# Sixteen neighbouring rows per partition: longer runs in HBM for a two-stage attention and highway kernel

## The chip, the cores and the metric

The kernel runs on one core of a Trainium2 chip. The metric is the device time of one execution in microseconds, the median of three runs. The core's engines are TensorE (PE, with its weight loads shown as PEld), VectorE (DVE), ScalarE (ACT), GpSimd (POOL) and SyncE (SP). Sixteen DMA engines move data between HBM and the on-chip memory; POOL and SP each issue transfers on a queue of their own.

## The reference

There are four batches of N = 6336 rows with C = 256 channels. Attention runs over channels, not over rows, so the score matrix of a batch is 256 x 256:

```python
qn = q / (norm(q, axis=1) + 1e-06)          # over the 6336 rows
kn = k / (norm(k, axis=1) + 1e-06)
s = kn.transpose(0, 2, 1) @ qn / tau        # 256 x 256 for each batch
a = softmax(s, axis=-1)
x = (v @ a).reshape(4 * 6336, 256)
H = maximum(x @ w_h, 0)
T = 1 / (1 + exp(-(x @ w_t + b_t)))
out = T * H + (1 - T) * x
```

The scores and the norms are sums over all rows of a batch. In the second half every row of v gives one row of the output, and no row depends on another.

## The kernel before

The rows of a batch are cut into 50 tiles of up to 128 rows, one row to a partition; the last tile has 64. Tiles are gathered into groups of `GS` = 16, so a batch has groups of 16, 16, 16 and 2 tiles. `_load_group` loads a group into an on-chip tile of 128 partitions x 16 x 256. The inputs are float32 and the on-chip tiles float16, and the transfer converts. For a full group it is one transfer of 2 MB read and 1 MB written. For the group of two tiles, one of which is not full, there is one transfer for each tile. All loads are issued on POOL's queue. The tiles of q and k have four buffers each, and those of v three.

A batch has three stages. Stage one (L120 to L149) runs over all tiles and adds up k'q, and the 128 x 128 diagonal blocks of k'k and q'q, in two PSUM banks: six matmuls for each tile. Stage two (L151 to L248) turns this into the normalized scores, their softmax and its product with the two weight matrices: short instructions that hand over between DVE, ACT and TensorE. Then the loads of q and k of the next batch and of its first v group are written (L250 to L252). Stage three (L254 to L395) takes the tiles in pairs. It transposes v on TensorE (L284), copies the transposed pair out of PSUM on DVE or ACT in turn (L296, L301), multiplies it with the prepared matrices (L329, L336, L343), and combines the results: a sigmoid and two rectifications on ACT (L354, L366), two subtractions on DVE (L370), a multiplication on POOL (L378) and a last subtraction on DVE (L382) into the output tile `ostg`, of which there are two buffers. The v load of a group is written one group ahead. A group's output goes out in two halves of `OGS` = 8 tiles: `_store_group` issues each as one transfer on SP's queue, and the last group's as one for each tile.

The order in which an engine runs its instructions is not that of the text alone: the framework (`TileContext`) orders each engine's instructions when the kernel is built, by its own estimate and by the order of the text, and puts in the semaphores. Each engine then runs its list in that order. POOL's list holds all load issues and the multiplications of stage three.

Of the kernel before, what the change touches and what calls it, by code (L numbers as in the profile page):

```python
# [15 lines left out]
P = 128  # L16
# [3 lines left out]
def kernel(  # L20
# [11 lines left out]
    nc = tc.nc  # L32
# [9 lines left out]
    def rows_of(s):  # L42
        return last_rows if s == nsub - 1 else P
# [4 lines left out]
    s = 0  # L48
    while s < nsub:
        ns = min(GS, nsub - s)  # L50
# [21 lines left out]
        out=wht[:, :, 0:C], in_=moe_w_h.rearrange("(kt jl) m -> jl kt m", kt=2)  # L72
    )
    nc.gpsimd.dma_start(
        out=wht[:, :, C : 2 * C], in_=moe_w_t.rearrange("(kt jl) m -> jl kt m", kt=2)
# [13 lines left out]
    def load_qk(bb):  # L89
        for gi, (s0, ns) in enumerate(groups):  # L90
            qt = stream_pool.tile(
                [P, ns, C], f16, tag="q_in", bufs=4, name=f"q{bb}_{gi}"
            )
            kt_ = stream_pool.tile(
                [P, ns, C], f16, tag="k_in", bufs=4, name=f"k{bb}_{gi}"
            )
            _load_group(nc, qt, q[bb], s0, ns, rows_of)
            _load_group(nc, kt_, k[bb], s0, ns, rows_of)
            q_tiles[(bb, gi)] = qt
            k_tiles[(bb, gi)] = kt_  # L100

    def load_v(bb, gi):
        s0, ns = groups[gi]
        vt = stream_pool.tile([P, ns, C], f16, tag="v_in", bufs=3,
                              name=f"v{bb}_{gi}")
        _load_group(nc, vt, v[bb], s0, ns, rows_of)
        v_tiles[(bb, gi)] = vt
# [4 lines left out]
    for b in range(B):  # L112
        ob = out[b * N : (b + 1) * N]
# [6 lines left out]
        for gi, (s0, ns) in enumerate(groups):  # L120
            qt = q_tiles.pop((b, gi))
            kt_ = k_tiles.pop((b, gi))
            for si in range(ns):
                s_idx = s0 + si
                nr = rows_of(s_idx)
# [33 lines left out]
        for idx, (c, off) in enumerate(  # L159
# [3 lines left out]
                out=junk[:, idx, :],  # L163
# [13 lines left out]
        for c in range(2):  # L177
            nc.vector.tensor_scalar(
                out=dcat[:, c, :],
# [12 lines left out]
        for c in range(2):  # L192
            nc.vector.scalar_tensor_tensor(
                out=t1[:, c, :],
# [10 lines left out]
            out=rs, in_=araw, axis=mybir.AxisListType.X, op=AluOp.add  # L205
# [3 lines left out]
        for c in range(2):  # L209
            nc.vector.tensor_scalar(  # L210
                out=mr[:, c, 0:C],
# [20 lines left out]
        for jk in range(2):  # L232
            nc.scalar.copy(
                out=at_sb[:, jk, :].rearrange("p (ic i) -> p ic i", ic=2),
                in_=atps[:, :, jk, :],
# [74 lines left out]
        for pi in range(len(pairs)):  # L310
            if pi + LOOKAHEAD < len(pairs):
                emit_transpose(pi + LOOKAHEAD)
            gi, s0, si, pn, nrows = pairs[pi]
            vt_sb = vtsb_tiles.pop(pi)
            ostg = ostg_tiles[gi]
            ns = groups[gi][1]
# [4 lines left out]
            for u in range(pn):  # L321
                nr = nrows[u]
# [32 lines left out]
                out=uu[0:nr0, 0:pn, :],  # L355
                in_=p3b[0:nr0, 0:pn, :],
# [7 lines left out]
            for u in range(pn):  # L364
                nr = nrows[u]
                nc.scalar.activation(  # L366
                    out=hh[0:nr, u, :], in_=p3a[u][0:nr, C : 2 * C],
# [3 lines left out]
                    out=dd[0:nr, u, :],  # L371
# [7 lines left out]
                out=pp[0:nr0, 0:pn, :], in0=uu[0:nr0, 0:pn, :],  # L379
# [3 lines left out]
                out=ostg[0:nr0, si : si + pn, :], in0=hh[0:nr0, 0:pn, :],  # L383
# [4 lines left out]
            if si + pn >= ns:  # L388
                o0 = 0
                while o0 < ns:  # L390
                    on = min(OGS, ns - o0)
                    _store_group(nc, ob, ostg, s0, o0, on, rows_of)
                    o0 += on
                del ostg_tiles[gi]
                v_tiles.pop((b, gi))  # L395


def _load_group(nc, tile_ap, src2d, s0, ns, rows_of):
    full = all(rows_of(s0 + i) == P for i in range(ns))
    if full:  # L400
        nc.gpsimd.dma_start(  # L401
            out=tile_ap[:, 0:ns, :],
            in_=src2d[s0 * P : (s0 + ns) * P, :].rearrange("(s p) c -> p s c", p=P),
        )
    else:
        for i in range(ns):
            nr = rows_of(s0 + i)
            nc.gpsimd.dma_start(
                out=tile_ap[0:nr, i, :],
                in_=src2d[(s0 + i) * P : (s0 + i) * P + nr, :],  # L410
            )


def _store_group(nc, dst2d, tile_ap, s0, o0, on, rows_of):
    full = all(rows_of(s0 + o0 + i) == P for i in range(on))
    base = (s0 + o0) * P
    if full:
        nc.sync.dma_start(
            out=dst2d[base : base + on * P, :].rearrange("(s p) c -> p s c", p=P),
            in_=tile_ap[:, o0 : o0 + on, :],  # L420
        )
    else:
        for i in range(on):
            nr = rows_of(s0 + o0 + i)
            nc.sync.dma_start(
                out=dst2d[base + i * P : base + i * P + nr, :],
                in_=tile_ap[0:nr, o0 + i, :],
            )

# [2 lines left out]
_INS = ['q', 'k', 'v', 'tau', 'moe_w_h', 'moe_w_t', 'moe_b_t']  # L432
_OUTS = [((25344, 256), 'float32')]
#: Inputs that are plain numbers.
_NUMBERS = {'tau': 1.0}


# [26 lines left out]
```

## Time and profile before

| | before |
|---|---|
| time, median of 3 runs | 414.38 us (414.25 to 415.24) |
| span of the profiled execution | 412.4 us, 6770 instructions |
| PE / PEld busy | 297.5 us (72%) / 212.1 us (51%) |
| DVE busy | 208.9 us (51%) |
| ACT busy | 183.3 us (44%) |
| POOL busy | 189.2 us (46%) |
| load queue (q0) | 77568 packets, 39.20 MB written |
| store queue (q1) | 25856 packets, 25.95 MB |

The profile is of one execution. For this execution it gives the span from the first to the last instruction, 412.4 us; its whole time is not recorded apart from the runs' median, which is 2.0 us longer than the span. Busy shares are means over stages that have different limits, so they don't say by themselves what sets the time. In the rows below, a line such as `93.17 0.61 PE L284 MATMUL vtps<-ident,v ... [10.51 <-DMA v<-in_v_dram]` says that at 93.17 us TensorE began matmuls of line 284, which read the tile `v`, after it had stood idle for 10.51 us, and that a transfer into `v` ended the wait.

### The profile page before, as it was taken

To read this page: it belongs to the slowest core of one execution; us is meant where nothing else is said; L and a number is where in the kernel's file an instruction comes from. 1 tells how busy PE (TensorE), PEld (TensorE's weight loads), DVE (VectorE), ACT (ScalarE), POOL (GpSimd) and SP (SyncE) were. 2 spreads that over 40 slices of the span, in tenths; PEclk is the share of its full clock that TensorE was granted. 3 is DMA by queue.
4 is the path that set the end of the run, shared out by engine and by line. 5 is a ranking of instruction groups with operands and counts; after the bars stand their busy time and mean duration, and the time that the engine had idled before them with its cause. 6 is when DMAs were issued, how large, how long until landed. Compare 5 with 4: busy or idle time off the path is not lost.

```text
span 412.4 us, 6770 instructions
## 1 busy us (share of the span) xinstructions
PE 297.5 (72%) x2637; PEld 212.1 (51%) x2637; DVE 208.9 (51%) x426; ACT 183.3 (44%) x407; POOL 189.2 (46%) x173
## 2 busy tenths in 40 slices
PE   0186839809877899968777999777778938776770
PEld 0176737506544698544445986444447815444440
DVE  0000103707876704497767232887766144786663
ACT  1000126605655306756555055566552166655561
POOL 9212322634646634555548441557366002754453
PEclk9999969957999999999999999999999968999996
DMA  7999999999962999999439999494329700433333
GB/s 95 198 199 197 198 198 199 197 233 188 195 193 70 217 245 198 197 222 241 124 103 173 238 205 198 94 209 138 109 67 215 163 0 0 113 102 103 103 102 121
DMA packets 103456, 65.57 MB, mean 159 GB/s; under 512 B 1537, under 2 KB 103425, under 8 KB 103425
## 3 DMA queue, kind: packets, MB, share of 16 engines
q0 software_dynamic: 77568, 39.20, 70.3%
q1 hardware_dynamic: 25856, 25.95, 20.6%
q8 instruction: 20, 0.33, 0.3%
q14 instruction: 12, 0.09, 0.1%
HBM read 78.38 MB, written 25.95 MB: 253 GB/s over the span
## 4 chain that ended last, share of the span: by engine, by line
PE 24%; DMA 24%; DVE 23%; POOL 17%; issue 7%; ACT 4%; POOLq 0%; DVEq 0%; ACTq 0%
POOL pp L378 15%; DVE o L382 14%; DMA k<-in_k_dram 14%; DVE dd L370 7%; PE p3a L336 7%; DMA v<-in_v_dram 6%; PE sg L129 5%; DMA q<-in_q_dram 4%; PE p3b L329 3%; PE sg L136 2%; PE sg L143 2%; PE vtps L284 2%; ACT hh L366 2%; PE p3b L343 1%; DVE vtsb L296 1%
## 5 line engine op out<-in xcount | busy, mean ns | idle before, releaser
L378 POOL TENSOR_TENSOR pp<-uu,dd 128x512 f32<-128x512 f32 (+1 forms) x104 | 131.4, 1273 | 144.0 <-DVE dd L370 64.8
L336 PE MATMUL p3a<-mr,vtsb 128*128 128x512 f16 (+1 forms) x400 | 134.7, 385 | 33.6 <-DVE dd L370 33.5
L382 DVE TENSOR_TENSOR o<-hh,pp 128x512 f32<-128x512 f32 (+1 forms) x104 | 94.4, 923 | 52.3 <-POOL pp L378 52.3
L366 ACT ACTIVATE hh<-p3a 128x256 f32<-128x256 f32 x200 | 76.1, 386 | 87.1 <-PE p3a L336 57.5
L129 PE MATMUL sg<-q,k 128*128 128x256 f16 (+1 forms) x400 | 94.7, 281 | 25.0 <-DMA k<-in_k_dram 24.1
L329 PE MATMUL p3b<-mr,vtsb 128*128 128x256 f16 (+1 forms) x400 | 100.3, 276 | 0.6 <-ACT uu L354 0.5
L370 DVE TENSOR_TENSOR dd<-hh,p3a 128x256 f32<-128x256 f32 x200 | 75.4, 413 | 29.2 <-ACT hh L366 29.0
L136 PE MATMUL sg<-k 128*128 128x128 f16 (+1 forms) x400 | 89.8, 225 | 0.0
L143 PE MATMUL sg<-q 128*128 128x128 f16 (+1 forms) x400 | 89.7, 224 | 0.0
L296 DVE CAST vtsb<-vtps 128x512 f16<-128x512 f32 (+1 forms) x52 | 34.5, 664 | 98.4 <-PE vtps L284 98.1
L284 PE MATMUL vtps<-ident,v 128*128 128x128 f16 (+1 forms) x400 | 41.1, 222 | 34.9 <-DVE vtsb L296 22.7
L336 PEld LDWEIGHTS <-vtsb 128*128 128x128 f16 (+1 forms) x400 | 39.3, 99 | 42.4 <-issue 18.9
L329 PEld LDWEIGHTS <-vtsb 128*128 128x128 f16 (+1 forms) x400 | 39.3, 99 | 42.2 <-issue 26.7
L354 ACT ACTIVATE uu<-p3b 128x512 f32<-128x512 f32 (+1 forms) x104 | 59.8, 579 | 0.1
L284 PEld LDWEIGHTS <-v 128*128 128x128 f16 (+1 forms) x400 | 30.8, 99 | 54.2 <-issue 32.6
L129 PEld LDWEIGHTS <-k 128*128 128x128 f16 (+1 forms) x400 | 40.2, 100 | 30.5 <-DMA k<-in_k_dram 29.9
L343 PE MATMUL p3b<-btb,ident 128*128 128x256 f16 x200 | 55.2, 276 | 0.0
L143 PEld LDWEIGHTS <-q 128*128 128x128 f16 (+1 forms) x400 | 40.2, 101 | 6.9 <-issue 1.1
L301 ACT CAST vtsb<-vtps 128x512 f16<-128x512 f32 (+1 forms) x52 | 29.3, 563 | 29.2 <-PE vtps L284 29.2
L153 ACT COPY ssb<-sg 128x512 f32<-128x512 f32 x8 | 4.3, 589 | 84.7 <-PE sg L143 84.7
L136 PEld LDWEIGHTS <-k 128*128 128x128 f16 (+1 forms) x400 | 40.2, 101 | 1.7 <-issue 1.4
L401 POOL DMA_DIRECT2D k<-in_k_dram x12 | 14.1, 1176 | 27.9 <-PE sg L143 23.5
(44 smaller groups left out, 123.2 us busy)
## 6 DMA issues: line engine op xcount, KB each, us to landing
out_dram<-o SPq DMA_DIRECT2D x24, 1024.0 KB, 5.4
q<-in_q_dram POOLq DMA_DIRECT2D x12, 1024.0 KB, 19.6
k<-in_k_dram POOLq DMA_DIRECT2D x12, 1024.0 KB, 17.4
v<-in_v_dram POOLq DMA_DIRECT2D x12, 1024.0 KB, 18.0
out_dram<-o SPq DMA_DIRECT2D x4, 128.0 KB, 9.6
q<-in_q_dram POOLq DMA_DIRECT2D x4, 64.0 KB, 23.1
k<-in_k_dram POOLq DMA_DIRECT2D x4, 64.0 KB, 22.6
v<-in_v_dram POOLq DMA_DIRECT2D x4, 64.0 KB, 4.5
```

The costliest lines, as they stand in the source:

```text
L129: nc.tensor.matmul(sg[c][:, 0:C], kt_[0:nr, si, bass.ts(c, P)], qt[0:nr, si, :], start=first, stop=False,)
L136: nc.tensor.matmul(sg[c][:, C : C + P], kt_[0:nr, si, bass.ts(c, P)], kt_[0:nr, si, bass.ts(c, P)], start=False, stop=False,)
L143: nc.tensor.matmul(sg[c][:, C + P : C + 2 * P], qt[0:nr, si, bass.ts(c, P)], qt[0:nr, si, bass.ts(c, P)], start=False, stop=last,)
L284: nc.tensor.matmul(vtps[:, u, c, 0:nr], vt_in[0:nr, si + u, bass.ts(c, P)], ident[0:nr, 0:nr], start=(pcnt == 0), stop=(pcnt == 2 * pn - 1),)
L329: nc.tensor.matmul(p3b[0:nr, u, :], vt_sb[:, u, kt, 0:nr], mr[:, kt, 2 * C : 3 * C], start=(kt == 0 and u == 0), stop=False,)
L336: nc.tensor.matmul(pa[0:nr, :], vt_sb[:, u, kt, 0:nr], mr[:, kt, 0 : 2 * C], start=(kt == 0), stop=(kt == 1),)
L343: nc.tensor.matmul(p3b[0:nr, u, :], ident[:, 0:nr], btb, start=False, stop=(u == pn - 1),)
L354: nc.scalar.activation(out=uu[0:nr0, 0:pn, :], in_=p3b[0:nr0, 0:pn, :], func=Act.Sigmoid, scale=-1.0,)
L366: nc.scalar.activation(out=hh[0:nr, u, :], in_=p3a[u][0:nr, C : 2 * C], func=Act.Relu,)
L370: nc.vector.tensor_tensor(out=dd[0:nr, u, :], in0=hh[0:nr, u, :], in1=p3a[u][0:nr, 0:C], op=AluOp.subtract,)
L378: nc.gpsimd.tensor_tensor(out=pp[0:nr0, 0:pn, :], in0=uu[0:nr0, 0:pn, :], in1=dd[0:nr0, 0:pn, :], op=AluOp.mult,)
L382: nc.vector.tensor_tensor(out=ostg[0:nr0, si : si + pn, :], in0=hh[0:nr0, 0:pn, :], in1=pp[0:nr0, 0:pn, :], op=AluOp.subtract,)
```

## The change

For a full group, partition p now holds the 16 neighbouring rows 16p to 16p + 15 of the group, where it held the rows p, 128 + p, 256 + p and so on. In HBM a partition's share of a load is then one run of 16 KB instead of 16 runs of 1 KB. A store still takes half of the tile, eight of the 16 slots, so each partition writes one run of 8 KB instead of eight of 1 KB. For that `_store_group` is given the group's size `ns`, and a store is contiguous only when the whole group is full. The group of two tiles keeps its transfers of one row to a partition. Tiles on the chip keep their shape and their names, and no instruction of TensorE, DVE or ACT is changed.

```diff
@@ -389,7 +389,7 @@
-                    _store_group(nc, ob, ostg, s0, o0, on, rows_of)
+                    _store_group(nc, ob, ostg, s0, ns, o0, on, rows_of)
@@ -400,7 +400,7 @@
         nc.gpsimd.dma_start(
             out=tile_ap[:, 0:ns, :],
-            in_=src2d[s0 * P : (s0 + ns) * P, :].rearrange("(s p) c -> p s c", p=P),
+            in_=src2d[s0 * P : (s0 + ns) * P, :].rearrange("(p s) c -> p s c", p=P),
         )
@@ -411,19 +411,20 @@
-def _store_group(nc, dst2d, tile_ap, s0, o0, on, rows_of):
-    full = all(rows_of(s0 + o0 + i) == P for i in range(on))
-    base = (s0 + o0) * P
+def _store_group(nc, dst2d, tile_ap, s0, ns, o0, on, rows_of):
+    full = all(rows_of(s0 + i) == P for i in range(ns))
     if full:
+        grp = dst2d[s0 * P : (s0 + ns) * P, :].rearrange("(p s) c -> p s c", p=P)
         nc.sync.dma_start(
-            out=dst2d[base : base + on * P, :].rearrange("(s p) c -> p s c", p=P),
+            out=grp[:, o0 : o0 + on, :],
             in_=tile_ap[:, o0 : o0 + on, :],
         )
     else:
         for i in range(on):
             nr = rows_of(s0 + o0 + i)
+            r0 = (s0 + o0 + i) * P
             nc.sync.dma_start(
-                out=dst2d[base + i * P : base + i * P + nr, :],
+                out=dst2d[r0 : r0 + nr, :],
                 in_=tile_ap[0:nr, o0 + i, :],
             )
```

## Rows read from the trace of the kernel before

**Rows 1.** The page, 40 slices: DMA share in tenths, GB/s moved

```profile
DMA  7999999999962999999439999494329700433333
GB/s 95 198 199 197 198 198 199 197 233 188 195 193 70 217 245 198 197 222 241 124 103 173 238 205 198 94 209 138 109 67 215 163 0 0 113 102 103 103 102 121
```

**Rows 2.** Chain that ended last, 0 to 140 us: start, us, what

```profile
9.44 30.47 DMA k<-in_k_dram
...
41.57 25.91 DMA k<-in_k_dram
...
67.78 25.34 DMA v<-in_v_dram
```

**Rows 3.** Stretches: length, busy us of each engine, PEclk, DMA share, GB/s

```profile
10.00:20.00 10.00, 1.22 (x9) 1.03 (x10) 0.00 (x0) 0.00 (x0) 2.82 (x5) 1.00 1.45 197
...
60.00:70.00 10.00, 8.69 (x95) 6.69 (x94) 3.61 (x10) 5.53 (x10) 2.33 (x2) 0.99 1.46 198
...
84.00:92.00 8.00, 0.00 (x0) 0.00 (x0) 0.00 (x0) 0.00 (x0) 1.92 (x2) 0.50 1.29 244
...
122.00:124.00 2.00, 1.73 (x13) 1.02 (x11) 1.21 (x3) 1.51 (x5) 0.80 (x2) 1.00 1.04 348
```

**Rows 4.** The page, DMA queues and HBM

```profile
q0 software_dynamic: 77568, 39.20, 70.3%
q1 hardware_dynamic: 25856, 25.95, 20.6%
q8 instruction: 20, 0.33, 0.3%
...
HBM read 78.38 MB, written 25.95 MB: 253 GB/s over the span
```

**Rows 5.** Waits from 0 to 100 us: total, times, longest

```profile
PE sg L129 <- DMA k<-in_k_dram: 24.1, 4, 12.3
...
PE vtps L284 <- DMA v<-in_v_dram: 10.5, 1, 10.5
```

**Rows 6.** TensorE's timeline: group 1, first and last of 96 matmuls; first behind v

```profile
29.37 0.28 PE L129 MATMUL sg<-q,k 128*128 128x256 f16 x1 [1.51 <-DMA k<-in_k_dram]
...
36.39 0.22 PE L143 MATMUL sg<-q 128*128 128x128 f16 x1
...
93.17 0.61 PE L284 MATMUL vtps<-ident,v 128*128 128x128 f16 x4 [10.51 <-DMA v<-in_v_dram]
```

**Rows 7.** POOL's timeline: start, us, instruction, count, [idle before <- releaser]

```profile
3.74 1.21 POOL L401 DMA_DIRECT2D q<-in_q_dram  x1
...
67.78 1.15 POOL L401 DMA_DIRECT2D v<-in_v_dram  x1 [3.93 <-DMA k<-in_k_dram]
...
79.86 1.21 POOL L401 DMA_DIRECT2D k<-in_k_dram  x1 [0.75 <-PE sg L136]
...
134.67 1.21 POOL L401 DMA_DIRECT2D v<-in_v_dram  x1
135.90 1.28 POOL L378 TENSOR_TENSOR pp<-uu,dd 128x512 f32<-128x512 f32 x1
...
345.41 1.26 POOL L378 TENSOR_TENSOR pp<-uu,dd 128x512 f32<-128x512 f32 x1 [28.35 <-ACT uu L354]
...
407.18 0.72 POOL L378 TENSOR_TENSOR pp<-uu,dd 64x256 f32<-64x256 f32 x1 [1.35 <-DVE dd L370]
```

**Rows 8.** Waits from 100 us to the end: total, times, longest

```profile
PE sg L129 <- DMA q<-in_q_dram: 0.7, 1, 0.7
...
PEld L284 <- DMA v<-in_v_dram: 0.2, 1, 0.2
```

**Rows 9.** Groups by line, POOL's issues: busy us, mean ns

```profile
L401 POOL DMA_DIRECT2D v<-in_v_dram x12 | 14.5, 1207 | 17.7 <-DMA q<-in_q_dram 9.8 <-PE p3b L343 4.0 <-DMA k<-in_k_dram 3.9
...
L408 POOL DMA_DIRECT2D v<-in_v_dram x8 | 4.6, 576 | 1.9 <-PE p3b L343 1.9
```

**Rows 10.** The page, DMA issues: count, KB each, us to landing

```profile
out_dram<-o SPq DMA_DIRECT2D x24, 1024.0 KB, 5.4
```

## The prediction

> **What bounds the kernel now.** I read the 40 slices of the page first. From the second to the eighth, some 10 to 82 us, the rate stands at 197 to 199 GB/s; after that it moves up and down [rows 1]. So the run has two parts. The chain that ended last says the same: from 9 to 93 us it consists of three long pieces that are waits for loads (30.5, 25.9 and 25.3 us), and the last of them is a v load [rows 2].
>
> The stretches give the rate. With loads alone it is 197 to 198 GB/s, and the DMA share doesn't move [rows 3]. These are bytes written as f16; HBM reads are 78.4 MB where the load queue moves 39.2 MB [rows 4], so the loads read about 396 GB/s. One load of a full group writes 1.049 MB and thus takes 1.049 / 0.198 = 5.30 us.
>
> Which load sets the end of this part? The waits of TensorE: until 100 us it waits 24.1 us for k in four waits (the longest, 12.3, ahead of the first matmul) and 10.5 us for v [rows 5]. That v wait ends at 93.17 us [rows 6], and in the 8 us before it no engine but POOL does anything [rows 3]. It is the v of group 1 of batch 0, issued at 67.78 us, the 15th full-group load in POOL's queue [rows 7], behind all of q and k of batch 1. Check: 15 loads of 5.30 are 79.5 us; the eight single-tile loads of the two last groups (0.39 MB) 2.0 us; one store that passes between them 3.4 us (84 to 92 us moved 244 GB/s, 1.95 MB; less a store of 1.05 that leaves 0.90 of loads where 1.58 would have passed alone, and the missing 0.68 MB are 3.4 us [rows 3]). That is 84.9 us; with the first issue at 3.74, 4.5 us remain for the weights, the first descriptors and the last landing. So the time of this landing is 15 times the time of one load plus about 13.6 us.
>
> After 100 us TensorE waits 0.7 us for q and its weight loads 0.2 us for v, in all [rows 8]. The other 320 us are matmuls and the chain of ACT, DVE and POOL, with loads far ahead. What the change gains or loses is therefore read between 4 and 93 us; later, loads and stores are covered by arithmetic.
>
> **The change part by part.** Bytes, instruction counts of the engines, tile shapes and waits stay: sums over rows don't care which partition holds which row, and v's rows go out in the order in which they came in. Only the runs in HBM change.
>
> *Loads.* A full group was 2048 runs of 1 KB and is 128 of 16 KB. The trace has no load of such runs, so I bound it by the nearest rows. The only packets of about that size are those of the instruction queue q8: 20 packets, 0.33 MB, 0.3% of 16 engines' span [rows 4]. Before rounding 0.25 to 0.35% of 16 x 412.4 us are 16.5 to 23.1 us, or 0.82 to 1.15 us a packet, 0.99 in the middle. The load queue had 77568 packets in 70.3%, 59.8 ns each, 0.957 us for sixteen. So by this row a load takes between 0.82 / 0.957 = 0.86 and 1.21 times its present time, 4.57 to 6.40 us. Parity is in the middle of that, but q8's few packets fell between those of the busy load queue and carry waits for it, while whatever a packet costs by itself is paid by the loads 2048 times and would be paid 128 times. I take the middle between parity and the favourable end, 0.93: 4.92 us. For 15 loads that is 15 x 0.38 = 5.7 us (bounds: 11.0 gained, 16.5 lost).
>
> [...]
>
> *Issues on POOL.* A full-group issue holds POOL 1.21 us, one of 128 or 64 runs 0.58 [rows 9]. If runs set this, each of 36 issues gets about 0.6 us shorter. Before the first load of the chain that is worth 0.6 us (bound: nothing, if descriptors are used while they are still written). Later it matters only where a multiplication of the third stage starts right behind an issue, as at 134.67 and 135.90 us [rows 7]; there are five such places, up to 3.0 us, but the multiplications behind them soon wait for DVE again. I take 0.5.
>
> *Stores.* Runs of 8 KB for 1 KB. A store is 5.4 us from issue to landing [rows 10], and where one passed alone the queues moved 348 GB/s [rows 3]. The buffer it empties is wanted two groups later; the 25 pairs of the last batch take from 345 to 408 us [rows 7], so a group of eight pairs is some 20 us. Nothing waits for them but the one that crosses the loads at 84 us (3.4 us, which could halve or vanish if the v load lands first; I take nothing). The last stores belong to the group of two tiles, which keeps its 1 KB rows. Cost and gain nothing; without the cover of the arithmetic one store would be worth its 3 us.
>
> *Queues.* POOL is the queue of all loads and of the multiplications; an issue there that blocks holds both. No wait is added. Behind the v load, the next late thing would be the v of group 2, wanted some 20 us later and issued at once behind it, with one k load between: 10 us, so it is not late.
>
> Sum: 5.7 + 0.6 + 0.5 = 6.8 us. The profiled span is 412.4 us, and the median of the runs 414.4: 2.0 us lie around the span and stay. 412.4 - 6.8 = 405.6, and 407.6 as a run.
>
> **Rivals.**
>
> *The runs stay short, or their length doesn't matter.* If the transfer is still cut at each row of 256 elements, nothing changes: 414.4. If runs are long but the read rate was at its limit, only POOL's 1.1 us remain: 413.3. For it: the load rate is so flat that it looks like a ceiling [rows 1, 3], and no row shows a higher one for reads. Against: a fixed cost of each packet gives a rate that is as flat. [...]
>
> *Long packets are slower* (the other side). If the middle of q8's row is right, a load takes 0.99 / 0.957 of 5.30 = 5.48 us, and 15 x 0.18 - 1.1 = 1.6 us are lost: 416.0; at its far end 6.40 us, 16.5 - 1.1 lost: 429.8. Place: the same v landing. It decides slower from 5.46 us a load (1.24 + 1.1 = 2.34 us over 15). For it: the row itself; against: its waits among the loads.
>
> *The order of instructions changes.* The framework orders each engine's work ahead of time: a k load of batch 2 stands at 79.86 us among the multiplications of batch 0 [rows 7], though the text has it a batch later. If its estimate of a load depends on runs, the order moves. TensorE stands idle for over 10 us before the v landing, and the 16 tiles of a group in stage one take 7.0 us (29.37 to 36.39) [rows 6]: one group of batch 1 moved into that gap would give 7 more, 400.6. The other way, work that now fills a wait moves out of it and the saving is eaten: 412 to 418.
>
> **How the numbers follow.** The trace speaks for the first part's bound and for little else, so most of the chance lies there; the row of q8, read at its middle, keeps the slow case alive, and for a change of the order no row gives a sign, only a place where it would pay more than it could cost. A load between 4.57 and 5.22 us in the present order: 0.62, about 402.3 to 412.1, likeliest 407.6 and mostly 404.5 to 410. No effect: 0.15. Slower packets: 0.08. A better order: 0.10. A worse one: 0.05. A measurement of this kernel tells 0.3%, 1.24 us, from no change. Faster: 0.62 + 0.10 = 0.72. Same: 0.15 + 0.02 of the worse order = 0.17. Slower: 0.11. The range of 402 to 414.4 us holds the first case, the second and little else, about 0.78.
>
> **What would show it.** The load rate between 10 and 80 us: right if near 213 GB/s, wrong if still 198 or below. Packets of the load queue: some 8,400 in place of 77,568 (36 x 128, the single-tile loads' rows, the weights and completions), and of the store queue some 4,400 in place of 25,856; if they stay, the runs were cut. POOL's issues near 0.6 us. The v wait of TensorE should end near 87 us, and everything behind it should stand about 6 us earlier in the same order; if the distance from that landing to the end is not some 319 us, the order or the third stage moved, and the sum is wrong there. TensorE's waits for loads after 100 us should stay below 1 us; if they grow, transfers I counted as covered aren't.

## The result, and the profile after

The changed kernel takes 402.94 us (median, 402.27 to 404.79) beside 414.31 us for the kernel before (414.04 to 415.24), measured together: a ratio of 0.973, 95% interval 0.970 to 0.976. That is 11.4 us faster, inside the range that was forecast, 4.7 us below the forecast time of 407.6 and below the stretch of 404.5 to 410 in which it was mostly expected. The profiled execution took 402.83 us; its span is 401.1 us, 11.3 less than before.

The page of the kernel after: the DMA share and rate in 40 slices, the load and store queues, HBM's bytes, and the stores' time from issue to landing.

```profile
DMA  7999999997726999993229996553259100322223
GB/s 117 215 217 212 213 217 215 214 263 149 251 105 138 302 212 212 220 276 118 109 57 255 264 217 130 141 176 115 106 108 287 47 0 0 116 105 108 105 105 124
...
q0 software_dynamic: 8448, 39.20, 49.5%
q1 hardware_dynamic: 4352, 25.95, 16.2%
...
HBM read 78.38 MB, written 25.95 MB: 260 GB/s over the span
...
out_dram<-o SPq DMA_DIRECT2D x24, 1024.0 KB, 4.7
```

The bytes are those of [rows 4], and the packets of the load queue fell from 77568 to 8448: the runs really are long. The flat part of the rate is there as in [rows 1], but at 212 to 217 GB/s.

Stretches of the kernel after (length, busy us of PE, PEld, DVE, ACT and POOL, granted clock, DMA share, GB/s):

```profile
10.00:20.00 10.00, 3.39 (x25) 2.89 (x26) 0.00 (x0) 0.00 (x0) 1.09 (x2) 1.00 1.02 214
...
60.00:70.00 10.00, 9.53 (x85) 6.63 (x83) 3.39 (x9) 6.59 (x14) 1.80 (x2) 1.00 1.05 219
...
84.00:92.00 8.00, 7.62 (x40) 4.68 (x41) 5.36 (x9) 3.38 (x8) 2.24 (x2) 0.63 1.03 237
```

Beside [rows 3] the loads' rate is 214 to 219 where it was 197 and 198, 215 in the mean from 10 to 80 us. A load of 1.049 MB so takes 4.88 us where it took 5.30. The third line shows what that did: from 84 to 92 us TensorE now works 7.62 us, where it stood still before.

The chain that ended last (start, us, what) and TensorE's waits up to 100 us (total, times, longest), after:

```profile
6.39 29.95 DMA k<-in_k_dram
...
37.39 24.80 DMA k<-in_k_dram
...
62.47 21.86 DMA v<-in_v_dram
```

```profile
PE sg L129 <- DMA k<-in_k_dram: 20.4, 3, 10.1
...
PE vtps L284 <- DMA v<-in_v_dram: 6.1, 1, 6.1
```

The same three loads hold the first part as in [rows 2]. The waits have shrunk from 24.1 to 20.4 us and from 10.5 to 6.1 us [rows 5]: the loads still set the end of this part, by less.

TensorE's timeline after, at its first matmul of stage one and at the end of the v wait:

```profile
16.61 0.39 PE L129 MATMUL sg<-q,k 128*128 128x256 f16 x1 [10.08 <-DMA k<-in_k_dram]
...
84.38 0.61 PE L284 MATMUL vtps<-ident,v 128*128 128x128 f16 x4 [6.14 <-DMA v<-in_v_dram]
```

The first matmul stood at 18.79 us before, the end of the v wait at 93.17 [rows 6]. So 2.18 us come before any matmul, 8.79 us are there by the v landing, and the last 2.5 of the 11.3 us arise behind it. To place those I use the matmul of L187, which runs once in stage two of every batch. It stood at 61.73, 158.63, 244.97 and 333.01 us before, and stands at 57.31, 149.74, 235.02 and 321.19 now. From the v landing to the second of them is 65.46 us before and 65.36 after; to the third 86.34 and 85.28; to the fourth 88.04 and 86.17; to the end 79.39 and 79.91. TensorE's timeline at the two ends of the middle stages, before and then after:

```profile
158.63 0.27 PE L187 MATMUL cqb<-dcat,ones2d 128*128 128x256 f16 x1
...
333.01 0.27 PE L187 MATMUL cqb<-dcat,ones2d 128*128 128x256 f16 x1
```

```profile
149.74 0.27 PE L187 MATMUL cqb<-dcat,ones2d 128*128 128x256 f16 x1
...
321.19 0.27 PE L187 MATMUL cqb<-dcat,ones2d 128*128 128x256 f16 x1
```

The two middle stages got 2.93 us shorter. TensorE waits for one load there, the q of [rows 8], before and not after:

```profile
250.65 0.27 PE L129 MATMUL sg<-q,k 128*128 128x256 f16 x1 [0.65 <-DMA q<-in_q_dram]
```

From one instruction to the same one in the kernel after, 0.62 of the 2.93 us are gained at this wait; where the rest is gained is seen under e4_long_early.

The last stage hides gains and a loss. The last store is issued 75.37 us behind L187 before and 74.33 after; it lands 3.10 us after its issue before and 2.52 after, behind the last store of 8 KB runs; and from there to the end of the span it is 0.92 us before and 3.02 after. What is waited for there is a DRAIN that GpSimd's queue runs at the end of the program. The last lines of the two kernels, L459 before and L460 after (count, ns min/median/max, first and last start):

```profile
L459 POOLq DRAIN  x3: 51/102/1972, 407.2 to 412.1; - x3
```

```profile
L460 POOLq DRAIN  x3: 51/102/5975, 394.3 to 400.8; - x3
```

The long one is the first of the three. Before, it ends at 409.13 us, 2.3 ahead of the last store's landing; after, it ends at 400.27, 2.2 behind that landing, and the closing instructions of all engines follow only then, from 400.32 us on. The change thus loses 2.1 us at the end of the run.

What is gained up to the v landing divides by the completions of the loads in the trace. From the first k load to the v of batch 1 (twelve full-group loads and the eight small ones) it is 65.62 us before and 61.30 after: 4.32. From there to the v load that ends the wait, with one store crossing, it is 8.76 us and 6.47: 2.29, of which 0.42 is one load's rate. The store's crossing itself thus costs 3.46 us before and 1.59 after.

The trace also has the completion of each of the 16 DMA engines, and what waits for a load starts with the last of them: the first matmul 0.05 us behind it before and 0.04 after (18.74 and 16.57 us at the first k load), the matmul behind the v wait 0.05 and 0.04 (93.12 and 84.34 us). By the mean of the 16, the first load completes at 12.36 us before and 11.33 after, the first k load at 17.64 and 16.19, and the v of batch 1 at 83.53 and 77.01. So from the k to that v 5.07 us are gained, 12 x 0.42, and 6.52 in all. The last engine trails the mean by 1.10 us before and 0.38 after at the first k load, and by 0.83 and 0.86 at that v: of the 2.18 us at the first matmul 0.7 are the last engine's and are lost again on the way, which is why the completions of the last engine give 4.32 and not 5.07.

### The profile page after: what moved, and what is told of

It is laid out like the page before. It is cut to its first block, busy times and chain, and to the rows that moved or that the text cites. A ratio compares the mean times of both kernels' runs of the same rounds, so it can differ in the third digit from the quotient of the medians.

```text
span 401.1 us, 6770 instructions
## 1 busy us (share of the span) xinstructions
PE 295.7 (74%) x2637; PEld 211.2 (53%) x2637; DVE 206.1 (51%) x426; ACT 183.6 (46%) x407; POOL 167.8 (42%) x173
## 3 DMA queue, kind: packets, MB, share of 16 engines
q0 software_dynamic: 8448, 39.20, 49.5%
## 4 chain that ended last, share of the span: by engine, by line
PE 30%; DVE 23%; DMA 19%; POOL 16%; issue 5%; ACT 5%; POOLq 0%; DVEq 0%; ACTq 0%
POOL pp L378 15%; DVE o L382 14%; DMA k<-in_k_dram 14%; PE sg L129 7%; DVE dd L370 7%; PE p3a L336 7%; DMA v<-in_v_dram 5%; PE sg L136 4%; PE sg L143 4%; PE p3b L329 3%; PE vtps L284 2%; ACT hh L366 2%; DVE vtsb L296 1%; PE p3b L343 1%; PE ahat L241 1%
## 5 line engine op out<-in xcount | busy, mean ns | idle before, releaser
L378 POOL TENSOR_TENSOR pp<-uu,dd 128x512 f32<-128x512 f32 (+1 forms) x104 | 132.5, 1283 | 146.2 <-DVE dd L370 68.3
L382 DVE TENSOR_TENSOR o<-hh,pp 128x512 f32<-128x512 f32 (+1 forms) x104 | 91.4, 895 | 52.2 <-POOL pp L378 52.2
L129 PE MATMUL sg<-q,k 128*128 128x256 f16 (+1 forms) x400 | 93.7, 279 | 20.8 <-DMA k<-in_k_dram 20.4
L370 DVE TENSOR_TENSOR dd<-hh,p3a 128x256 f32<-128x256 f32 x200 | 75.6, 414 | 28.3 <-ACT hh L366 28.3
L343 PEld LDWEIGHTS <-ident 128*128 128x128 f16 x200 | 19.7, 99 | 3.9
```

The source lines that it names most:

```text
L129: nc.tensor.matmul(sg[c][:, 0:C], kt_[0:nr, si, bass.ts(c, P)], qt[0:nr, si, :], start=first, stop=False,)
L343: nc.tensor.matmul(p3b[0:nr, u, :], ident[:, 0:nr], btb, start=False, stop=(u == pn - 1),)
L370: nc.vector.tensor_tensor(out=dd[0:nr, u, :], in0=hh[0:nr, u, :], in1=p3a[u][0:nr, 0:C], op=AluOp.subtract,)
L378: nc.gpsimd.tensor_tensor(out=pp[0:nr0, 0:pn, :], in0=uu[0:nr0, 0:pn, :], in1=dd[0:nr0, 0:pn, :], op=AluOp.mult,)
L382: nc.vector.tensor_tensor(out=ostg[0:nr0, si : si + pn, :], in0=hh[0:nr0, 0:pn, :], in1=pp[0:nr0, 0:pn, :], op=AluOp.subtract,)
```

## The experiments

Theory A is that the load rate sets the time to the v landing, that the stores are covered, and that whatever is gained later comes from POOL's shorter issues. The expectations name the rivals. Every kernel was timed beside the kernel before on the same chip; "before" is 414.0 to 414.4 us in each case.

### Loads alone, stores alone

Kernel before with long loads only, and kernel after with its loads put back. In these two, in e3_long_late, e4_long_early and e13_first_two_short loads and stores place some rows differently, so rows of the output stand at other places; bytes and instruction counts are the same.

```diff
# e1_long_loads: before, in _load_group
-            in_=src2d[s0 * P : (s0 + ns) * P, :].rearrange("(s p) c -> p s c", p=P),
+            in_=src2d[s0 * P : (s0 + ns) * P, :].rearrange("(p s) c -> p s c", p=P),
# e2_long_stores: after, in _load_group
-            in_=src2d[s0 * P : (s0 + ns) * P, :].rearrange("(p s) c -> p s c", p=P),
+            in_=src2d[s0 * P : (s0 + ns) * P, :].rearrange("(s p) c -> p s c", p=P),
```

> All full-group loads in 16 KB runs, stores as before in 1 KB rows, so rows of v leave at other places than they should. Theory A (the saving is made by the loads: 6.3 us of load rate and 1.3 us of the start before the v landing, 2.5 us of shorter issues on POOL after it, and 1.2 us where the one store crosses the loads): 403 to 404.5 us, the v wait ends at 84.5 to 86 us, and 316.7 us follow it. Theory B (the 2.5 us after the landing come from the stores' longer runs): 405.5 us or more, and 319 us follow the landing.

Measured: 403.37 us (401.79 to 404.75), ratio 0.975 (0.972 to 0.977). That can't be told from the whole change's 402.94. The v wait ends at 83.10 us, 1.3 earlier than with long stores as well and earlier than Theory A had it; 316.9 us follow it, Theory A's figure. The waits of TensorE up to 160 us:

```profile
PE vtps L284 <- DMA v<-in_v_dram: 4.9, 1, 4.9
```

> All loads in 1 KB rows as before, the stores of full groups in 8 KB runs (v's rows leave at other places). Theory A: at most the crossing of one store is saved, 413 to 414.5 us, the v wait ends at 92 to 93.2 us and 319 us follow it. Theory B: 411.8 us, with some 316.7 us behind the landing.

Measured: 411.94 us (411.41 to 412.43), ratio 0.994 (0.993 to 0.996): 2.2 us faster, more than Theory A's bound and Theory B's figure, but not at Theory B's place: the two middle stages together are 0.3 us shorter than before, with the wait for q gone. The wait for v ends at 92.38 us, 0.8 earlier than before, and the last stage of the profile takes 77.84 us for 79.39: 0.6 less from the issue of the last store to its landing (2.53 for 3.10) and 1.0 less up to that issue.

The 0.6 recurs: that landing takes 2.51 to 2.53 us in every kernel here with stores of 8 KB runs and 3.10 to 3.12 in every one with 1 KB alone. The 1.0 goes with TensorE's clock. Around the last L187 its granted clock falls to 0.50, from 333.2 us on in the kernel before, after TensorE worked for 1.25 of 4 us (329 to 333 us). Where the clock rests there for 6.8 to 8.5 us behind L187, it is 74.1 to 74.8 us to the last store's issue, and where it rests for 9.4 to 10.8 us, 75.3 to 75.5. Kernels with loads and stores of 1 KB runs alone behind the v landing stand on both sides (before 10.2 us, e7 and e11 6.8), so nothing shows that the runs set it, and that part of the 2.2 us is open, as is 1.0 us of the whole change's gain.

What follows: long loads alone bring the whole effect, and long stores add nothing beside them that these runs can show, though they bring 2.2 us beside short loads. The two effects don't add. One reason is seen at the crossing of the store with the v load, read as before from the completions less one load's own time:

```
store run, load run    from v of batch 1 to the late v, less one load
1 KB, 1 KB (before)    8.76 - 5.30 = 3.46 us
8 KB, 1 KB (e2)        7.83 - 5.30 = 2.53
8 KB, 16 KB (after)    6.47 - 4.88 = 1.59
1 KB, 16 KB (e1)       5.19 - 4.88 = 0.31
```

With the store's runs unchanged, longer runs of the load lower the price (3.46 to 0.31, and 2.53 to 1.59). Longer runs of the store lower it beside loads of 1 KB and raise it beside loads of 16 KB. Other kernels with the first pair of lengths have 3.50 and 3.51 us (e3, e7), with the last pair 0.73 and 0.13 (e4, e13). Among long loads a store of short runs is the one that yields: in e1 it lands 19.1 us after its issue, in the kernel after 11.1, and nothing waits for it.

### Late loads alone, early loads alone

Kernel before; long runs only for the loads that come after the v landing, or only for those up to it:

```diff
-            _load_group(nc, qt, q[bb], s0, ns, rows_of)
-            _load_group(nc, kt_, k[bb], s0, ns, rows_of)
+            # e3_long_late; e4_long_early has bb < 2
+            _load_group(nc, qt, q[bb], s0, ns, rows_of, long=bb >= 2)
+            _load_group(nc, kt_, k[bb], s0, ns, rows_of, long=bb >= 2)
...
-        _load_group(nc, vt, v[bb], s0, ns, rows_of)
+        # e4_long_early: in, not "not in"
+        _load_group(nc, vt, v[bb], s0, ns, rows_of, long=(bb, gi) not in ((0, 0), (0, 1), (1, 0)))
```

> Only the loads behind the 15th are in 16 KB runs (all of batches 2 and 3, and v from group 2 of batch 0 and from group 1 of batch 1 on); stores in 1 KB rows, so some rows leave at other places. Theory A: the v wait still ends near 93.1 us, POOL's later issues fall to 0.6 us, some 316.7 us follow the landing, 411.8 us. Theory B (issues on POOL are covered later on): 414.3 us, 319 us follow.

Measured: 410.63 us (410.45 to 411.03), ratio 0.992 (0.990 to 0.993): 3.5 us faster, with the v wait ending at 94.20 us, 1.0 later than before. The two middle stages together take 171.34 us; they took 174.38 before and take 171.45 after. The last stage of the profile is 1.2 us shorter than before, all of it ahead of the last store's issue, with 6.8 us at the lower clock.

> Only the first 15 loads (q and k of batches 0 and 1, v of group 0 of both and of group 1 of batch 0) are in 16 KB runs; stores in 1 KB rows, so some rows leave at other places. Theory A: the v wait ends at 84.5 to 86 us, 319 us follow it, 405 to 407.5 us. Theory B: about the same landing, and 316.7 us behind it, 402.5 to 404.5 us, as nothing behind the landing hangs on the later loads.

Measured: 404.29 us (403.12 to 404.90), ratio 0.976 (0.973 to 0.978). The v wait ends at 84.18 us, as after; the two middle stages take 173.83 us, 0.55 less than before, and what is gone there is the wait for q. The time lies in Theory B's range and not in Theory A's, because the v wait ended 0.3 us ahead of Theory A's and the last stage took 78.3 us, 1.1 less than before; the middle stages speak for Theory A.

What follows: the two halves of the gain lie where the theory puts them, some 9 us ahead of the v landing and some 3 behind it, and the second half needs nothing but long runs of the late loads. How their shorter issues act is seen on DVE where a load is issued, at 134.67 us [rows 7]. DVE's timeline, before:

```profile
134.38 0.42 DVE L370 TENSOR_TENSOR dd<-hh,p3a 128x256 f32<-128x256 f32 x1 [0.29 <-ACT hh L366]
134.72 3.02 DVE L382 TENSOR_TENSOR o<-hh,pp 128x512 f32<-128x512 f32 x2
137.66 1.07 DVE L370 TENSOR_TENSOR dd<-hh,p3a 128x256 f32<-128x256 f32 x3
```

TensorE's timeline, before, the matmul that waits for this:

```profile
138.12 0.38 PE L336 MATMUL p3a<-mr,vtsb 128*64 128x512 f16 x1 [1.54 <-DVE dd L370]
```

The same place in the kernel after, on POOL, DVE and TensorE:

```profile
126.40 0.59 POOL L401 DMA_DIRECT2D v<-in_v_dram  x1
127.02 1.28 POOL L378 TENSOR_TENSOR pp<-uu,dd 128x512 f32<-128x512 f32 x1
```

```profile
126.45 2.40 DVE L382 TENSOR_TENSOR o<-hh,pp 128x512 f32<-128x512 f32 x2
128.78 0.74 DVE L370 TENSOR_TENSOR dd<-hh,p3a 128x256 f32<-128x256 f32 x2
```

```profile
129.24 0.38 PE L336 MATMUL p3a<-mr,vtsb 128*64 128x512 f16 x1 [0.92 <-DVE dd L370]
```

Read it from POOL: the multiplication L378 starts right behind the issue, at 135.90 us before and 127.02 after, and so ends 0.62 us earlier counted from the issue's start. DVE's second subtraction L382 ends some 0.55 us behind that multiplication in both kernels (137.74 less 137.18; 128.85 less 128.30), the next L370 stands behind it in DVE's list, and TensorE waits for that L370: 1.54 us before, 0.92 after. Nothing between takes the 0.62 us up again. There are five such places in the kernel before (134.67, 177.98, 221.46, 265.98 and 309.41 us), and by the starts of DVE's instructions on either side of them they gained 0.62, 0.43, 0.70, 0.70 and 0.62 us, 3.07 in all. In e1_long_loads and e3_long_late the same five gained the same, in e4_long_early 0.06 at most. Of the 2.93 us in the two middle stages, 2.45 are four of these places and 0.62 the wait for q, less 0.14 lost between. The first place lies ahead of these stages, behind the v landing, where 0.5 us are lost again within 8 us; there the granted clock rests at 0.50 for 5.5 us behind the landing, where it did for 4.5 before. In e3_long_late, whose first part is as before, the same two subtractions take as long as after:

```profile
135.80 2.40 DVE L382 TENSOR_TENSOR o<-hh,pp 128x512 f32<-128x512 f32 x2
```

### Runs between 1 KB and 16 KB

Kernel after with RUN = 4 and with RUN = 2 neighbouring rows to a run, in loads and stores; in the load:

```diff
-            out=tile_ap[:, 0:ns, :],
-            in_=src2d[s0 * P : (s0 + ns) * P, :].rearrange("(p s) c -> p s c", p=P),
+            out=tile_ap[:, 0:ns, :].rearrange("p (a r) c -> p a r c", r=RUN),
+            in_=src2d[s0 * P : (s0 + ns) * P, :].rearrange(
+                "(a p r) c -> p a r c", p=P, r=RUN
+            ),
```

> Four neighbouring rows to a run, in loads and stores: 4 KB in HBM, 512 runs for a load. Theory A (each packet has a fixed cost beside its bytes, from 5.30 us at 1 KB and 4.88 us at 16 KB a load: 0.45 us x 1/4 of it remains at 4 KB): a load takes 4.96 us, a rate of 211 GB/s, POOL's issue 0.68 us, 404 to 405.5 us. Theory C (the rate is a matter of whether a partition's whole share is one run): 198 GB/s and 412 us or more.

Measured: 407.28 us (406.41 to 407.86), ratio 0.983 (0.980 to 0.987), slower than expected. The v wait ends at 88.32 us. A stretch (columns as above):

```profile
20.00:30.00 10.00, 9.92 (x113) 8.91 (x112) 0.00 (x0) 0.00 (x0) 1.52 (x2) 1.00 1.12 212
```

> Two neighbouring rows to a run, in loads and stores: 2 KB in HBM, 1024 runs for a load. Theory A: half of the fixed cost is left, a load takes 5.08 us, 206 GB/s, POOL's issue 0.85 us, 406.5 to 409 us. Theory C: 198 GB/s and 413 us or more.

Measured: 409.26 us (409.02 to 410.15), ratio 0.989 (0.985 to 0.992). The v wait ends at 90.42 us. The same stretch:

```profile
20.00:30.00 10.00, 9.13 (x100) 8.13 (x98) 0.00 (x0) 0.00 (x0) 1.01 (x2) 1.00 1.24 207
```

What follows: the load time is 5.30, 5.07, 4.95 and 4.88 us at runs of 1, 2, 4 and 16 KB. For each of the 16 engines that is, in the mean, 128, 64, 32 and 8 packets of a load. From the two ends, 0.42 us over 120 packets are 3.5 ns a packet; that gives 5.08 and 4.96 us in the middle, beside 5.07 and 4.95. So what the long runs save goes with the number of packets, as a fixed cost of each would, and Theory C is out. POOL's issue takes 1.17 to 1.21 us at 2048 runs, 0.90 to 0.94 at 1024, 0.76 to 0.80 at 512 and 0.55 to 0.58 at 128.

Why e5 was slower than expected: by the rate alone its v wait would end 15 x 0.07 = 1.1 us later than after, and it ends 3.9 us later. The crossing cost it 7.85 - 4.95 = 2.90 us, 1.3 more than after; its first matmul came at 17.79 us, 1.2 later. The expectation had neither.

### The start of the run

e7_first_two is the kernel before with long runs for the first q and k loads alone. e13_first_two_short is e4_long_early with short runs for these two alone.

```diff
# e7_first_two, before (the load of v keeps long=False)
+            _load_group(nc, qt, q[bb], s0, ns, rows_of, long=(bb, gi) == (0, 0))
+            _load_group(nc, kt_, k[bb], s0, ns, rows_of, long=(bb, gi) == (0, 0))
# e13_first_two_short, e4_long_early
-            _load_group(nc, qt, q[bb], s0, ns, rows_of, long=bb < 2)
-            _load_group(nc, kt_, k[bb], s0, ns, rows_of, long=bb < 2)
+            _load_group(nc, qt, q[bb], s0, ns, rows_of, long=bb < 2 and (bb, gi) != (0, 0))
+            _load_group(nc, kt_, k[bb], s0, ns, rows_of, long=bb < 2 and (bb, gi) != (0, 0))
```

> Only the first two loads (q and k of group 0 of batch 0) are in 16 KB runs, everything else as before. In the changed kernel the first matmul came 2.2 us earlier, of which the rate of two loads explains 0.8. Theory A (the rest is won because POOL writes the descriptors of the first six loads faster, and the engines are slow while it writes): the first matmul waits until 17.5 to 18 us, and the v landing moves by 0.8 to 1.2 us: 413 to 413.6 us. Theory D (the rest belongs to these two loads themselves): the first matmul at 16.6 us, the v landing 2.2 us earlier, 412 us.

Measured: 413.70 us (412.34 to 414.73), ratio 0.998 (0.996 to 1.000). The first matmul stands at 18.74 us and the v wait ends at 93.16, as before. The time is just above Theory A's; the matmul and the wait no theory had. The completions show why the first two loads' 0.84 us don't appear: by the mean of the 16 engines the first k load completes at 16.38 us, 1.26 earlier than before, but the last engine trails the mean by 2.32 us, where it trailed by 1.10. In this run the engines' completions of one load lie 2.85 us apart, where they lie 1.5 to 1.6 us apart before; in the kernel after it is 0.8 to 0.9 in the first six loads and 1.3 to 1.5 in the next eight. Here the distance stays as it was set at the start: the v of batch 1 completes 1.25 us earlier than before by the mean, and 0.05 by the last engine.

> The run with the first 15 loads in 16 KB runs, but for the first two, which keep 1 KB rows; stores in 1 KB rows, so some rows leave at other places. Theory E (the first landing is set by how POOL writes the first two loads' 2048 descriptors each, and everything behind keeps that offset): the first matmul waits until 18.2 to 18.9 us, the v landing comes 1.4 to 2 us later than in that run, at 85.6 to 86.2 us, 405.5 to 406.5 us. Rival F (the offset is set by the loads behind them, or by chance): the first matmul at 16.6 to 17.8 us, and the v landing at most 0.9 us later.

Measured: 404.90 us (404.49 to 405.20), ratio 0.977 (0.975 to 0.979), 0.6 us above e4_long_early. The first matmul stands at 17.94 us, between what the theories gave, and the v wait ends at 84.39 (e4: 84.18). Rival F's bound of a small effect fits. By the mean, though, the first k load completes at 17.58 us, 1.35 later than in e4_long_early and as with short runs throughout, which is Theory E's place.

What follows: the runs of the first two loads move the engines' mean by 1.3 us, in e7 and e13 alike, and the time by 0.6 at most, since the last engine's distance from the mean differs from run to run. Of the 2.18 us at after's first matmul 0.84 is the rate, 0.7 the last engine's distance, and 0.6 is there at the first load already. That is the size of the first issue's gain (1.21 to 0.57 us), but that it is the issue isn't shown: with 4 and 2 KB runs the issues are shorter than before as well, and the first load's mean completion is 12.38 and 12.81 us. Kernels whose first loads all have 16 KB runs had their first matmul between 16.56 and 17.05 us in five profiles and at 18.52 in one (e12_v2_ahead below); with 1 KB runs throughout it stood between 18.39 and 18.91. By the engines' mean the first k load completes at 16.16 to 16.28 us in all six and at 17.58 to 17.72 in the others.

### The late v load taken out of the way

If a single v landing holds the second part, moving that load should free more. e8_v_first is the kernel after with the v of group 1 issued ahead of the next batch's q and k; e9_v_behind_group0 moves only the load that is waited for, behind the first q and k of batch 1; e11_short_v_behind is the same move in the kernel before; e12_v2_ahead is e9 with the next v load moved as well.

```diff
# e8_v_first, after; in all four the text's later load of the same tile is skipped
         if b + 1 < B:
+            load_v(b, 1)
             load_qk(b + 1)
...
-                if gi + 1 < len(groups):
+                if gi + 1 < len(groups) and (b, gi + 1) not in v_tiles:
                     load_v(b, gi + 1)
# e9_v_behind_group0 (after) and e11_short_v_behind (before), in load_qk behind q and k of a group
+            if bb == 1 and gi == 0:
+                load_v(bb - 1, 1)
# e12_v2_ahead: e9, and
-            load_v(b + 1, 0)
+            b and load_v(b + 1, 0)
...
-                    load_v(b, gi + 1)
+                    load_v(b, gi + 1); b == 0 and gi == 1 and load_v(1, 0)
```

> The changed kernel, with the v load of group 1 of each batch written ahead of the q and k loads of the next batch. Theory A (the landing of this v load sets the end, and the rest hangs on it): the v load lands some 30 us earlier, the wait of 6.1 us for it is gone, and the gap is filled with the third stage of batch 0; then q and k of batch 1 land one load (4.9 us) later, before they are wanted. 393 to 399 us. Rival (the loads of q and k of batch 1 set the end as soon as v doesn't): 401 to 404 us, with the waits of TensorE moved to k.

Measured: 410.48 us (408.22 to 412.00), ratio 0.991 (0.988 to 0.994): faster than before, but slower than after and outside both ranges. TensorE's waits up to 160 us:

```profile
PE sg L129 <- DMA k<-in_k_dram: 31.9, 5, 10.7
```

The v wait is gone and the waits for k have grown from 20.4 to 31.9 us. The instruction order changed on TensorE, DVE, ACT and POOL: q and k loads of batch 2 that after issues at 75.44 and 94.60 us are issued at 132.86 and 133.44. The prediction's rival of a changed order came true here, so this run doesn't test the v landing alone.

> The changed kernel, with one load moved: the v load of group 1 of batch 0 goes out right behind q and k of group 0 of batch 1, ahead of six large and four small loads that are wanted much later. The lists of DVE, ACT and SP are the same, and TensorE's list is the same but for names. Theory A (the landing of this load sets the end, and all behind it hangs on it): TensorE's wait of 6.1 us for v is gone and with it the matmuls at half clock around it, 394 to 397.5 us, cqb of batch 1 near 142 us. Rival (as in the run before, where v was moved ahead of all of them: another load becomes the late one): 400 us or more, and the waits of TensorE for k grow by as much.

Measured: 398.27 us (397.41 to 400.63), ratio 0.963 (0.959 to 0.967), a little above what was expected. The other engines keep after's order. TensorE's waits up to 160 us:

```profile
PE sg L129 <- DMA k<-in_k_dram: 20.3, 4, 10.1
...
PE vtps L284 <- DMA v<-in_v_dram: 2.2, 1, 2.2
```

The wait of 6.1 us is gone, and 2.2 us have come up for the v of group 2, at 97.74 us.

> The kernel before, all runs of 1 KB, with the same one load moved. Theory A: TensorE's wait of 10.5 us for v is gone: 401 to 404 us. The distance to the run with long runs and the same move is then what long runs are worth when that landing is not late: 4.4 us up to the landing of the first k of batch 1 and 3 us of shorter issues, 6.5 to 8 us, in place of 11.4. Rival: 408 us or more, as the k loads of batch 1 are late in its place.

Measured: 413.97 us (412.11 to 414.31), ratio 1.000 (0.998 to 1.001), where 401 to 404 was expected. TensorE's waits up to 160 us:

```profile
PE vtps L284 <- DMA v<-in_v_dram: 11.2, 1, 11.2
```

The wait wasn't removed; it moved to the v of group 2, at 111.92 us. With short runs the loads have no room: what is read ahead of it stays on the queue ahead of it. So here Theory A failed in one point: before isn't held by the order of one load, but by all that passes the engines up to some 112 us, and that includes stores. Three stores cross the last three loads up to that landing and cost them 12.5 us beside their own time; in e9_v_behind_group0 the same three loads lose 6.1. So of the 14.2 us between the two landings (111.92 and 97.74) some 7.1 are the rate of 17 loads and 6.3 the crossings. With this move made, long runs are worth 413.97 - 398.27 = 15.7 us.

> The run with v of group 1 moved behind group 0, and also v of group 2 of batch 0 ahead of v of group 0 of batch 1, in the place that this load had. Theory A (in the first 100 us the loads are the bound, and what is late is whichever load is wanted soonest behind the queue): the wait of 2.2 us for v of group 2 goes, and nothing else becomes late: 395 to 397 us. Rival (two late stores or another load take its place): 398 us or more, with a wait of TensorE for a transfer of 2 us or more behind 60 us.

Measured: 396.53 us (396.46 to 396.59), ratio 0.957 (0.955 to 0.959), the best version, ahead of both kernels. From 54 us on no wait of TensorE ends with a load; up to there one is left (waits from 54 to 395 us have none, the last ends at 53.69):

```profile
53.69 0.40 PE L129 MATMUL sg<-q,k 128*128 128x256 f16 x1 [7.14 <-DMA k<-in_k_dram]
```

## Why the prediction was right, and where its sizes were off

*Bound and place: right.* The v landing sets the first part, before and after, and the order of instructions stayed. Loads are faster at long runs, and the time fell.

*Loads, 5.7 us: right, a little small, 6.3.* The load took 4.88 us, not 4.92, and 15 x 0.42 are 6.3; the mean of the engines shows 12 x 0.42 between the first k load and the v of batch 1. The row of q8, which could have meant a loss, meant nothing, but not for the reason given: its packets don't carry waits for the loads, as those with nothing else under way (928 and 933 ns, before) took as long as the others (879 to 1032). The loads' packets of 16 KB took 625 ns in the median; why those of q8 take longer isn't shown. That a packet has a cost of its own no row of before shows; the loads at runs of 2 and 4 KB agree with one (5.07 and 4.95 us measured, 5.08 and 4.96 estimated at 3.5 ns a packet).

*First issue, 0.6 us: right in size.* The first load is issued at 3.75 us, where it was at 3.74 [rows 7], and the sixth already at 6.39, where the chain of before has it at 9.44 [rows 2]. By the engines' mean the first load completes 1.03 us earlier, 0.42 by the rate and 0.6 by the start, and these 0.6 are still there at the v of batch 1 (6.52 less 14 x 0.42). That they come from the issue isn't shown.

*Later issues, 0.5 us: the step that failed.* The sentence that "the multiplications behind them soon wait for DVE again" took it that DVE was independent of them. It is not: at these places DVE's subtraction ends some 0.55 us behind the multiplication, the next L370 stands behind the subtraction, and TensorE waits for it. All of the bound, 3.0 us, was to be had: the five places gained 3.07 between the profiles, and the same in e3_long_late.

*Stores, nothing: too small by 1.9 us at one place and 0.6 at another.* The crossing was named, with 3.4 us that "could halve", and taken as nothing; it fell from 3.46 to 1.59. But long stores didn't do that: long loads did, and with short stores they lose only 0.13 to 0.73. The last stores keep 1 KB rows, as said, but the last of them lands 0.6 us sooner behind a store of 8 KB runs. Elsewhere stores are covered: in the kernel after TensorE waits for no transfer that the profile names after 100 us.

*What the sum didn't have.* The wait for q at 250.65 us, read in [rows 8] and then left alone, gave 0.6 us. The DRAIN at the end took 2.1 us back; in the kernel before it is hidden, as it ends ahead of the last store's landing.

*The sum.* 6.8 forecast, +0.6 loads, +2.6 later issues, +1.9 crossing, +0.6 last store, +0.6 wait for q, +1.0 up to the last store's issue (at the shorter stretch of lower clock, see e2_long_stores), -0.7 lost between the v landing and the last L187, -2.1 DRAIN are 11.3, the difference of the spans. So the sum missed 7.3 us of gain and 2.8 of loss, and that the time came out inside the range owes something to luck. The forecast of 87 us for the v landing was 84.38, and the 319 us behind it are 316.7. The packets, the issues' 0.6 us and the order were as forecast; the rival that the runs stay cut fell with the 8448 packets.

## What to carry to other kernels

Where loads alone hold a part of the run, read the rate there and the packets of the queue: at equal bytes, runs of 16 KB took 8% off a load of 1 KB runs here, and most of that was had at 4 KB (0.35 of 0.42 us). An issue on an engine that also computes is no side matter: look up what stands behind it in every list, down to the engine that ends the stage, before you call it covered. A transfer freed by a faster queue shows the next one in line, so move loads only after the rate is there: the same move was worth nothing with short runs, and 4.7 us with long ones (402.94 - 398.27). And compare the ends of the two spans as well: a cost that was hidden behind the last store can come out when all else gets shorter.

## What the runs showed of the hardware

*VectorE's long subtractions mostly end 0.55 us behind a multiplication of GpSimd.* Away from any issue, after, DVE and POOL:

```profile
107.27 1.74 DVE L382 TENSOR_TENSOR o<-hh,pp 128x512 f32<-128x512 f32 x1 [0.72 <-POOL pp L378]
...
109.26 0.68 DVE L382 TENSOR_TENSOR o<-hh,pp 128x512 f32<-128x512 f32 x1
```

```profile
105.97 2.50 POOL L378 TENSOR_TENSOR pp<-uu,dd 128x512 f32<-128x512 f32 x2 [1.14 <-DVE dd L370]
```

The first of these subtractions has its inputs at 107.27 us and takes 1.74 us where the next takes 0.68; it ends 0.54 us behind POOL's second multiplication (108.47). Both of its inputs lie on the chip in SBUF. L370, with one input in PSUM, takes its usual 0.42 us while a multiplication runs (before, at 133.68 us, inside the multiplication from 133.46 to 134.73). That the place of the inputs makes the difference isn't shown. Of the 24 subtractions of the kernel before that took over 0.9 us, 20 end 0.55 or 0.56 us behind a multiplication. Not all that overlap one are long: the one at 140.37 us took 0.68 us, inside a multiplication that took 1.86 (from 139.77 us) where the mean is 1.27. Whether POOL's issue also lengthens the subtraction isn't settled. At 134.72 us the first of the two ran in 0.68 us during an issue; the second began while POOL was still issuing, 0.58 us ahead of the multiplication at 135.90, and took 2.41 us all the same (DVE, before):

```profile
135.32 2.41 DVE L382 TENSOR_TENSOR o<-hh,pp 128x512 f32<-128x512 f32 x1
```

*What a store costs the load that it crosses depends on the runs of both.* The same megabyte of store cost that load between 0.13 and 3.51 us, by the lengths of the two runs. Why isn't shown.

*A load is as late as the last of its 16 engines, and their distance differs from run to run.* The first matmul starts 0.05 us behind the last completion before and 0.04 after, and 1.15 and 0.42 behind the mean. Completions of one load lie 1.3 us apart after, 2.85 us in e7_first_two, and in e3_long_late 1.5 us in the first loads and 2.6 from the fifth on. This is as large as what the first loads' runs could bring, so a single profile of the start tells little.

*GpSimd's DRAIN at the end is longer behind long runs.* It took 5.97 us in the five kernels with 16 KB runs in all full-group loads, 4.58 where only the loads behind the v landing have them (e3), 3.12 and 3.04 at 2 and 4 KB, and 1.97 us in all others, e4_long_early among them. Why isn't shown.
